# Products of constants ahead of waiting matmul groups in an attention stage with two MLPs

## The chip, the core and the metric

The kernel runs on one core of a Trainium2 chip. The metric is the device time of one execution in microseconds. A core has a tensor engine (matmul; PE in the rows, PEld for its weight loads), a vector engine (DVE), a scalar engine (ACT), a Pool engine (POOL) and a sync engine (SP), which here issues all DMAs. Matmuls write to PSUM, eight banks of 128 x 512 fp32; everything else works from SBUF. The tensor engine's clock is granted to it at one of two levels, 1.2 or 2.4 GHz.

## What is computed

Attention with normalised q and k over 4 batches, 12 heads, 448 positions and head size 64; then two MLPs on the 1792 x 768 result, the first with a squared ReLU and the second with a PReLU, each 768 to 2048 to 768.

```python
q_n, k_n = rmsnorm(q, g_q), rmsnorm(k, g_k)
scores = (1.0 / np.sqrt(64)) * np.matmul(q_n, k_n.transpose(0, 1, 3, 2))
scores = scores - np.max(scores, axis=-1, keepdims=True)
attn = np.exp(scores)
attn = attn / (np.sum(attn, axis=-1, keepdims=True) + 1e-09)
x = np.matmul(attn, v)          # brought to 1792 x 768
h = np.maximum(x @ moe_w_in, 0.0)
x = h * h @ moe_w_out
h = x @ moe2_w_in
g = np.maximum(h, 0.0) + moe2_alpha * np.minimum(h, 0.0)
return g @ moe2_w_out
```

## The kernel before

Most matmul operands are split into a high and a low part, and three products of parts stand for one fp32 product; a few products, L727 among them, are plain fp32 and run as two records each.

The order of all instructions is made by a planner, class Tasks. Every step is a task with its engine or engines, a cost in us for each, the buffers that it reads and writes, and an urgency. Tasks.run works out for each engine the task that could start soonest, by dependencies (plus a fixed delay, WAIT), by when the engine is done, and by when a buffer slot from the task's pool becomes free; among those within 0.05 us of the soonest the lowest urgency wins. Tasks marked with a gap start 0.12 us later on the vector and scalar engines. Steps of the vector engine that are not marked "free" share a port with the Pool engine in the plan, and exclude each other. The task chosen is emitted at once, so the planner's order is the program order on each engine. A slot is returned when the last task on its buffer has been emitted, with the planned end as the time from which it is free. Costs are simple formulas, such as 0.07 + 0.00104 n us for a vector operation on n columns, 0.05 + 0.00084 n for a scalar one that reads PSUM, and MM = 0.202 us for a product of 448 columns.

The attention stage (with_attention, L419) has six PSUM banks in the pool "bank" and two in "pv". It runs batches 0 and 1 with the first MLP of batches 0 and 1 woven in, then batches 2 and 3. Two of the six banks go over to the MLP's accumulators (give, L800; pool "m") once the first batch's last head has begun. The second function, without (L824), does the rest and is a planner run of its own.

In a batch, norms makes the reciprocal norms, rhl. For each pair of heads, spread (L626) brings them to all rows by a product into a bank (L634), one for k and one for q, and multiplies k or q in that bank (L639). prep (L661) copies each head's half of the bank to st (k) and mv (q) with the scalar engine (recorded at L254) and writes the low part with a subtraction on the vector engine (recorded at L262); four of these steps of each head read the two banks. shift (L677) makes four products per head into fresh banks (L683), reduces each to the row maximum mc (L687), transposes it (L690) and sends it by DMA into a row of mv. head (L697) makes the scores (L708) into fresh banks, takes the exponential (L716) into pf or hl, and multiplies with v into a bank of "pv" (L727, or L751 for the pairs in IN_PARTS); for L751 the low part hl is a subtraction that reads the scores' bank (L742, recorded at L262). norm (L758) divides: z and d are copied out of the pv bank, z by the scalar engine (L764) from one half of the partitions, d from the other (L767, recorded at L258 or L254).

columns is a 128 x 2 tile of constants, -1e-9 and 0 or -1, written at the start. The weight stream (single, L268 on) gives the vector engine steps on ws (L286 to L296), which are spread over the same time.

Of the kernel before, what the change touches and what calls it, by code (L numbers as in the profile page):

```python
# [16 lines left out]
B, H, S, D = 4, 12, 448, 64  # L17
# [8 lines left out]
NSEL = max(max(g) for g in GROUPS)  # L26
UP, DN = 384, 512
TINY = 2.0 ** -15

# [3 lines left out]
class Buf:  # L35


    def __init__(self, ap=None, pool=None):
        self.ap, self.pool, self.slot = ap, (pool,) if isinstance(pool, str) else pool, None
        self.left, self.open, self.until = 0, False, 0.0  # L40
        self.writer, self.readers = {}, {}
# [11 lines left out]
class Tasks:  # L53
# [2 lines left out]
    PRICE = {"A": 1.5, "V": 3.5, "P": 1.5}  # L56

    def __init__(self):
        self.phase = 0
        self.new, self.free, self.ends, self.last = [], {}, {e: 0.0 for e in "TAVPS"}, {}  # L60
        self.dma = self.port = 0.0
        self.gap = dict.fromkeys("TAVPS", 0.0)
# [4 lines left out]
    def add(self, urgency, on, emit, reads=(), writes=(), chain=None, after=None, free=False, off=False):  # L67

        deps, bufs = set(), []
        for kind, items in (("r", reads), ("w", writes)):
            for x in items:
                b, part = x if isinstance(x, tuple) else (x, None)
                if b not in bufs:
                    bufs.append(b)
                if part in b.writer:
                    deps.add(b.writer[part])
                if kind == "w":  # L80
                    deps.update(b.readers.get(part, ()))
        behind = [self.last[chain]] if chain in self.last else []
        if after:
            behind.append(after)
        t = Task(urgency, on, emit, bufs, deps, behind, {"P"} if free else {"P", "V"},
                 0.12 * off)
        t.phase = self.phase
        if chain:
            self.last[chain] = t
        for x in reads:  # L90
            b, part = x if isinstance(x, tuple) else (x, None)
            b.readers.setdefault(part, []).append(t)
        for x in writes:
            b, part = x if isinstance(x, tuple) else (x, None)
            b.writer[part], b.readers[part] = t, []
        for b in bufs:
            b.left += 1
        self.new.append(t)
        return t

    def run(self, phase=0):
        ready = {e: [] for e in self.ends}
        mine, self.new = [t for t in self.new if t.phase <= phase], [t for t in self.new if t.phase > phase]

        def offer(t):
            for e in t.on:
                ready[e].append(t)

        for t in mine:
            for d in (*t.deps, *t.behind):  # L110
                if d.start is None:
                    t.missing += 1
                    d.next.append(t)
        for t in mine:
            if not t.missing:
                offer(t)
        left = len(mine)
        while left:
            best = None
            for e, tasks in ready.items():  # L120
                found, soonest = [], None
                for t in tasks:
                    s = self.ends[e] + (max(t.gap, self.gap[e]) if e in "AV" else 0)
                    s = max(s, self.port) if e in t.alone else s
                    for d in t.deps:
                        s = max(s, d.end + (0 if d.engine == e == "T" else self.WAIT[e]))
                    for d in t.behind:
                        s = max(s, d.start)
                    taken = []
                    for b in t.bufs:  # L130
                        if b.ap is None:
                            taken.append(self.slot(b, taken))
                            s = max(s, taken[-1][0] + self.WAIT[e]) if taken[-1] else None
                            if s is None:
                                break
                    if s is None:
                        continue
                    if len(t.on) > 1:
                        other = min(max(self.ends[o], s, self.port if o in t.alone else 0) + self.PRICE[o] * t.on[o]
                                    + 0.7 * sum(x.on[o] for x in ready[o] if x.urgency < t.urgency)  # L140
                                    for o in t.on if o != e)
                        if s + self.PRICE[e] * t.on[e] > other + 0.2:
                            continue
                    found.append((s, t.urgency, t))
                    soonest = s if soonest is None else min(soonest, s)
                if found:
                    s, _, t = min((x for x in found if x[0] <= soonest + 0.05), key=lambda x: x[1])
                    if best is None or s < best[0]:
                        best = (s, e, t)
            assert best, "no task can start"  # L150
            s, e, t = best
            for o in t.on:
                ready[o].remove(t)
            for b in t.bufs:
                if b.ap is None:
                    _, n, b.pool = self.slot(b)
                    slots = self.free[b.pool]
                    b.slot = slots.pop(next(i for i, x in enumerate(slots) if x[1] == n))
                    b.ap = b.slot[2]
            t.engine, t.start = e, s  # L160
            if e == "S" and t.on[e]:
                self.ends[e] = s + 0.06
                self.dma = max(self.dma, s + 1.3) + t.on[e]
                t.end = self.dma + 0.8
            else:
                t.end = self.ends[e] = s + t.on[e]
                self.gap[e] = t.gap
                if e in t.alone:
                    self.port = t.end
            t.emit(e)  # L170
            left -= 1
            for b in t.bufs:
                b.left -= 1
                b.until = max(b.until, t.end)
                self.release(b)
            for n in t.next:
                n.missing -= 1
                if not n.missing:
                    offer(n)
# [19 lines left out]
def dve2(n):  # L199
    return 0.07 + 0.00052 * n  # L200
# [18 lines left out]
def attention_relu2_mlp_prelu_mlp(ctx: ExitStack, tc: tile.TileContext, qkt, qk_tm, v, gb, alpha, ident, sel,  # L219
                                  w1, w2, w3, w4, out):  # L220
    nc = tc.nc
    ts = Tasks()
# [11 lines left out]
    columns = const.tile([128, 2], F32, name="columns")  # L234
# [33 lines left out]
    def single(w, i, urgency, after=None, last=None):  # L268
# [14 lines left out]
        if last:  # L283
            last[:] = t0, t1
        add(urgency, {"V": dve2(n)},
            lambda e: nc.vector.tensor_scalar(out=f.ap[:, :n], in0=f.ap[:, :n], scalar1=TINY, scalar2=None, op0=ALU.max),  # L286
            [], [f])
# [131 lines left out]
    def with_attention():  # L419
        with ExitStack() as es:  # L420
# [61 lines left out]
            def constants(after):  # L482
# [2 lines left out]
                add(200, {"V": 0.1}, lambda e: nc.vector.tensor_scalar(out=al_b.ap, in0=al_b.ap, scalar1=-1.0, scalar2=None,  # L485
                                                                       op0=ALU.mult), [], [al_b])

            first_scores, qk_load = {}, [None]

            def attention(b, base, first=False):  # L490
# [328 lines left out]
            for u in range(cur[0], cur[0] + 3):  # L819
                prepare(u, 5000)  # L820
                made[u].open = True
            ts.run()

    def without():  # L824
        with ExitStack() as es:
# [353 lines left out]
    with tc.manual_schedule():  # L1179
        with_attention()  # L1180
        without()
# [64 lines left out]
```

## Time and profile before

| | us |
|---|---|
| median of 3 runs | 1263.94 |
| lowest and highest | 1261.74, 1265.78 |
| the profiled execution | 1261.38 |
| its span, first to last instruction | 1259.6 |
| tensor engine busy | 1177.3 |
| vector engine busy | 908.8 |
| scalar engine busy | 794.5 |

The mean granted clock of the profiled execution was 0.977 of full. Attention fills the stretch up to about 545 us. A line of the timeline gives start, length, engine, source line, operation, output and inputs, shape, count, and in brackets the idle time of that engine before it with the releaser. Merged lines cover several instructions in a row, and lengths of matmuls overlap a little. The chain of waits is followed back from the last instruction, so that its pieces lie end to end.

### The profile page before, as it was taken

What the parts mean: (1) busy time and instruction counts of PE and PEld (TensorE: products, weight loads), DVE (VectorE), ACT (ScalarE), POOL (GpSimd) and SP (SyncE); (2) the same over time, 40 slices, a digit from 0 to 9 for tenths busy, and PEclk for the clock granted to TensorE, in tenths of its full rate; (3) what the DMA queues carried; (4) which work ended last, traced back from release to release, by engine and by line L of the source; (5) the groups of instructions that cost most, each with busy time, mean ns of one, the idle gap of its engine ahead of it and who ended that gap; (6) DMA issues with size and microseconds to landing.
All of it is one profiled execution on the core that took longest, in us unless ns stands there. A gap on an engine that the chain in (4) does not pass through costs nothing.

```text
span 1259.6 us, 17375 instructions
## 1 busy us (share of the span) xinstructions
PE 1177.3 (93%) x5502; PEld 1016.9 (81%) x5502; DVE 908.8 (72%) x1632; ACT 794.5 (63%) x1596; POOL 527.3 (42%) x485
## 2 busy tenths in 40 slices
PE   4996999897999999999999999999999979999998
PEld 2554767686888888889989999888889879888988
DVE  6789999999988877613777661088777996847484
ACT  5687879787789978822555221376746755645472
POOL 4344355555555524310000003864777743317355
PEclk7997999898999999999999999999999989999999
DMA  6136657798645633358998996572617448161632
GB/s 189 55 117 218 226 192 252 253 309 296 241 150 167 221 132 121 110 182 269 315 335 296 340 358 215 187 266 92 236 62 263 160 162 252 57 201 50 204 110 88
DMA packets 95803, 250.32 MB, mean 199 GB/s; under 512 B 11296, under 2 KB 30880, under 8 KB 95712
## 3 DMA queue, kind: packets, MB, share of 16 engines
q1 hardware_dynamic: 95712, 249.22, 58.6%
q8 instruction: 43, 0.70, 0.2%
q14 instruction: 48, 0.39, 0.1%
HBM read 178.32 MB, written 70.78 MB: 198 GB/s over the span
## 4 chain that ended last, share of the span: by engine, by line
PE 63%; DVE 17%; ACT 9%; DMA 6%; issue 4%; SPq 1%; POOL 0%; ACTq 0%; DVEq 0%; POOLq 0%
PE n L982 26%; PE m L350 14%; PE bank L350 10%; PE bank L708 4%; PE pv L751 4%; PE pv L727 3%; DMA raw<-in_w 3%; DVE mc L687 2%; PE bank L683 2%; DVE ws L293 2%; DVE ws L296 2%; DVE n L993 1%; DMA whl<-w 1%; DVE ws L286 1%; DMA tm<-in_qk_tm 1%
## 5 line engine op out<-in xcount | busy, mean ns | idle before, releaser
L982 PE MATMUL n<-forms,whl 128*128 128x448 f32 x1008 | 212.1, 371 | 17.2 <-ACT ws L254 7.2
L982 PEld LDWEIGHTS n<-forms,whl 128*128 128x128 f32 x1008 | 190.7, 190 | 37.6 <-DVE forms L262 8.2
L350 PE MATMUL bank<-xs,whl 128*128 128x448 f32 x576 | 138.4, 373 | 1.1 <-DMA whl<-w 1.1
L350 PE MATMUL bank<-hg,whl 128*128 128x448 f32 x576 | 130.5, 370 | 2.6 <-DMA whl<-w 1.9
L982 PE MATMUL n<-xs,whl 128*128 128x448 f32 x576 | 124.2, 369 | 4.0 <-DMA whl<-k_u 2.8
L282 ACT ACTIVATE ws<-raw 128x384 f32<-128x384 f32 (+1 forms) x112 | 67.3, 601 | 95.3 <-DMA raw<-in_w 84.7
L982 PEld LDWEIGHTS n<-xs,whl 128*128 128x128 f32 x576 | 109.1, 190 | 14.1 <-DMA whl<-k_u 3.2
L350 PE MATMUL m<-xs,whl 128*128 128x448 f32 x576 | 118.0, 366 | 1.6 <-DMA whl<-w 0.9
L350 PEld LDWEIGHTS bank<-hg,whl 128*128 128x128 f32 x576 | 109.1, 191 | 12.7 <-DMA whl<-w 2.2
L350 PEld LDWEIGHTS bank<-xs,whl 128*128 128x128 f32 x576 | 108.6, 191 | 12.9 <-DMA whl<-w 1.7
L687 DVE TENSOR_REDUCE mc<-bank 112x1 f32<-112x448 f32 x192 | 111.5, 616 | 8.8 <-PE bank L683 7.5
L350 PEld LDWEIGHTS m<-xs,whl 128*128 128x128 f32 x576 | 107.9, 188 | 11.7 <-ACT q L254 1.1
L350 PE MATMUL m<-hg,whl 128*128 128x448 f32 x576 | 116.9, 365 | 0.0
L262 POOL TENSOR_TENSOR whl<-ws,whl 128x384 fp32r<-128x384 f32 (+2 forms) x57 | 80.5, 1422 | 83.3 <-ACT whl L254 61.1
L350 PEld LDWEIGHTS m<-hg,whl 128*128 128x128 f32 x576 | 108.2, 188 | 8.6
L262 POOL TENSOR_TENSOR whl<-raw,whl 128x384 fp32r<-128x384 f32 (+1 forms) x87 | 89.9, 1037 | 50.8 <-ACT whl L254 42.8
L262 POOL TENSOR_TENSOR xs<-q,xs 128x448 fp32r<-128x448 f32 x11 | 13.3, 1213 | 229.1 <-DMA q<-y 226.8
L708 PE MATMUL bank<-mv,st 128*128 128x448 f32 (+2 forms) x352 | 100.8, 392 | 6.5 <-DVE hl L262 2.9
L286 DVE TENSOR_SCALAR ws<-ws 128x384 f32<-128x384 f32 (+1 forms) x112 | 47.6, 427 | 81.7 <-ACT ws L282 81.5
L254 ACT ACTIVATE whl<-raw 128x384 fp32r<-128x384 f32 (+1 forms) x123 | 60.7, 500 | 56.0 <-PE n L982 43.1
L982 PE MATMUL n<-xt,whl 128*128 128x448 f32 x432 | 93.7, 366 | 1.7 <-DVE q L993 1.2
L262 DVE TENSOR_TENSOR hl<-bank,hl 128x448 fp32r<-128x448 f32 (+1 forms) x120 | 73.8, 619 | 27.8 <-ACT bank L716 25.4
(172 smaller groups left out, 2373.0 us busy)
## 6 DMA issues: line engine op xcount, KB each, us to landing
raw<-in_w SPq DMA_DIRECT2D x64, 384.0 KB
raw<-in_w SPq DMA_DIRECT2D x48, 512.0 KB
whl<-w SPq DMA_DIRECT2D x64, 384.0 KB
whl<-w SPq DMA_DIRECT2D x48, 512.0 KB
k_u<-whl SPq DMA_DIRECT2D x56, 384.0 KB
whl<-k_u SPq DMA_DIRECT2D x56, 384.0 KB
w<-whl SPq DMA_DIRECT2D x32, 384.0 KB
w<-whl SPq DMA_DIRECT2D x24, 512.0 KB
```

The costliest lines, as they stand in the source:

```text
L254: nc.scalar.activation(out=o, in_=i, func=ACTF.Copy)
L262: (nc.gpsimd if e == "P" else nc.vector).tensor_tensor(out=o, in0=x, in1=hi, op=ALU.subtract)
L282: lambda e: nc.scalar.activation(out=f.ap[:, :n], in_=half(1).bitcast(F32), func=ACTF.Abs), [raw], [f], "f")
L286: lambda e: nc.vector.tensor_scalar(out=f.ap[:, :n], in0=f.ap[:, :n], scalar1=TINY, scalar2=None, op0=ALU.max),
L293: lambda e: nc.vector.scalar_tensor_tensor(out=fu(), in0=half(1), scalar=0xC0000000, in1=fu(), op0=ALU.bitwise_and, op1=ALU.bitwise_or), [ ...
L296: lambda e: nc.vector.scalar_tensor_tensor(out=fu(), in0=half(0), scalar=29, in1=fu(), op0=ALU.logical_shift_right, op1=ALU.bitwise_or), [ ...
L350: nc.tensor.matmul(out=acc.ap[:, t, :S], lhsT=w.ap[:, part * n + 128 * kk:part * n + 128 * kk + 128], rhs=src(h, k0 + kk, t)[1](), start=( ...
L687: lambda e, t=t, pm=pm: nc.vector.reduce_max(out=mc.ap[:, t:t + 1], in_=pm.ap[:CP, :S], axis=AX.X),
L708: nc.tensor.matmul(out=pa.ap[:keys, :S], lhsT=s.ap[:rows, k, c:c + keys], rhs=m.ap[:rows, k, :], start=(k == 0), stop=(k == 1))
L727: lambda e, n=n, pfv=pfv, keys=keys: nc.tensor.matmul(out=o.ap[:, :S], lhsT=vs[p].ap.bitcast(F32)[:keys, 192 * n + 64 * j:192 * n + 64 * j ...
L751: nc.tensor.matmul(out=o.ap[:, :S], lhsT=l, rhs=r, start=(n == 0 and x == 0), stop=(half and x == 1))
L982: nc.tensor.matmul(out=psum(x), lhsT=w.ap[:, part * n + 128 * kk:part * n + 128 * kk + 128], rhs=get(h)[1](), start=fresh and h == 1, stop ...
```

## The change

The planner calls a function fill just before it emits a task of the tensor engine, if the planned start lies more than 1.5 us after the planned end of that engine's last task. The function looks whether the task has just taken a slot of the pools bank or pv. If so it issues products of the constants tile with itself into that slot: two columns on the stationary side, 448 moving columns that repeat the same two, plain fp32, two output rows. There are as many as fit into the planned gap less 0.6 us at 0.76 us each, or at 1.52 us ahead of the very first task. Their results are not read, and the group that follows starts its own accumulation in the same bank. Nothing is removed or moved; fill is switched off before the second function runs.

```diff
+FILL_LEAST, FILL_REST = 1.5, 0.6
...
-        self.phase = 0
+        self.phase, self.fill = 0, None
...
+            fresh = [b for b in t.bufs if b.ap is None]
             for b in t.bufs:
                 if b.ap is None:
                     _, n, b.pool = self.slot(b)
                     slots = self.free[b.pool]
                     b.slot = slots.pop(next(i for i, x in enumerate(slots) if x[1] == n))
                     b.ap = b.slot[2]
+            if e == "T" and self.fill and s - self.ends[e] > FILL_LEAST:
+                self.fill(fresh, self.ends[e], s)
             t.engine, t.start = e, s
...
+            def fill(bufs, since, until):
+                bank = next((b for b in bufs if b.pool in ("bank", "pv")), None)
+                if bank:
+                    for _ in range(int((until - since - FILL_REST) / (0.76 if since else 1.52))):
+                        nc.tensor.matmul(out=bank.ap[:2, :S], lhsT=columns, rhs=columns[:, None, :].to_broadcast([128, S // 2, 2]),
+                                         start=True, stop=True)
+
+            ts.fill = fill
...
             ts.run()
+            ts.fill = None
```

## Rows read from the trace of the kernel before

**Rows 1.** The page: busy time of each engine, and granted clock in 40 slices.
```profile
PE 1177.3 (93%) x5502; PEld 1016.9 (81%) x5502; DVE 908.8 (72%) x1632; ACT 794.5 (63%) x1596; POOL 527.3 (42%) x485
...
PEclk7997999898999999999999999999999989999999
```
**Rows 2.** Waits of PE, 0 to 660 us: waiter, releaser, total us, times, longest.
```profile
PE bank L634 <- DVE rhl L549: 7.9, 1, 7.9
PE bank L683 <- DVE mc L687: 6.2, 2, 5.9
...
PE bank L683 <- POOL mv L256: 3.7, 2, 2.1
PE bank L708 <- DVE mc L687: 3.1, 4, 2.2
...
PE bank L708 <- DVE hl L262: 2.9, 2, 2.6
PE bank L683 <- DVE hl L262: 2.5, 1, 2.5
```
**Rows 3.** Stretches: busy us (count) of PE, PEld, DVE, ACT, POOL; clock; DMA.
```profile
12.00:18.00 6.00, 0.00 (x0) 0.00 (x0) 5.78 (x11) 4.69 (x9) 0.00 (x0) 0.76 0.84 243
...
24.00:30.00 6.00, 4.67 (x11) 2.75 (x12) 5.92 (x13) 2.45 (x8) 0.56 (x1) 0.50 0.10 39
30.00:36.00 6.00, 6.00 (x21) 3.70 (x20) 4.09 (x10) 1.95 (x6) 0.00 (x0) 0.82 0.01 2
...
120.00:126.00 6.00, 4.93 (x17) 4.15 (x18) 5.23 (x10) 2.19 (x5) 1.18 (x2) 0.64 0.55 190
```
**Rows 4.** Chain of waits from 0 to 60 us: start, length, engine, line, count.
```profile
54.06 3.02 PE pv L727 x8
```
**Rows 5.** Timeline of PE, 0 to 130 us, the first long waits.
```profile
4.80 3.35 PE L527 MATMUL bank<-pf,hg 128*128 128x448 f32 x4 [4.80 <-ACT pf L520]
8.67 1.77 PE L527 MATMUL bank<-pf,hg 128*128 128x448 f32 x4 [0.51 <-ACT pf L520]
18.38 1.83 PE L634 MATMUL bank<-rhl,selg 128*128 128x448 f32 x4 [7.93 <-DVE rhl L549]
22.31 1.46 PE L683 MATMUL bank<-st,mv 128*112 128x448 f32 x3 [2.11 <-POOL mv L256]
```
**Rows 6.** The chain again, at half clock and, the last two, at full.
```profile
18.38 0.72 PE bank L634
...
28.73 2.24 PE bank L708 x6
30.97 0.75 PE bank L683 x2
31.71 1.05 PE pv L727 x2
...
57.49 0.81 PE bank L683 x4
58.30 1.31 PE bank L708 x6
```
**Rows 7.** Timeline of all engines around the wait that ends at 121.07 us.
```profile
108.67 1.05 PE L634 MATMUL bank<-rhl,selg 128*128 128x448 f32 x4 [0.93 <-DVE rhl L262]
...
112.84 1.15 DVE L262 TENSOR_TENSOR st<-bank,st 64x448 fp32r<-64x448 f32 x2
...
121.07 1.16 PE L683 MATMUL bank<-st,mv 128*112 128x448 f32 x2 [11.34 <-DVE st L262]
```
**Rows 8.** Waits of all engines, 105 to 126 us: the weight load of the second L683.
```profile
PEld bank L683 <- DVE mv L262: 0.2, 1, 0.2
```
**Rows 9.** Timeline of DVE: the first and the last of 23 operations in a row.
```profile
108.56 0.56 DVE L293 SCALAR_TENSOR_TENSOR ws<-raw,ws 128x384 uint32<-128x384 uint32 x1
...
120.30 0.63 DVE L262 TENSOR_TENSOR st<-bank,st 64x448 fp32r<-64x448 f32 x1
```
**Rows 10.** Timeline of all engines, 0 to 40 us: d behind z.
```profile
36.66 0.62 DVE L258 COPY d<-pv 64x448 f32<-64x448 f32 x1 [1.49 <-ACT z L764]
```

## The prediction

> **What bounds the kernel now.** I read the page's busy shares and slices first [rows 1]. The tensor engine is busy for 93% of the span, so what the change can win lies where its clock is down; the slices put that into the first 320 us, where the digits of the granted clock fall to 7 and 8. Next I read who the tensor engine waits for while attention runs [rows 2]: a few long waits, and the column to look at is the releaser, because the change treats all waits alike and the releasers are of two kinds. "L634 <- DVE rhl" and "L683 <- POOL mv" are waits for an operand. "L683 <- DVE mc", "L708 <- DVE mc", "L708 <- DVE hl" and "L683 <- DVE hl" are waits for a bank: mc is what the reduction of L687 writes and hl what the subtraction of L742 writes, and a product of L683 or L708 reads neither; both only read a PSUM bank that the next product needs. Third, the clock by stretches [rows 3]: it stands at 0.50, the lower of its two levels (1.2 and 2.4 GHz), from about 15 us until 32.2 us (0.82 over 30 to 36 is 2.2 us at half), and again from the wait that ends at 121.07 us until 124.3 us (0.64 over 120 to 126 is 28%, 1.7 us, at full).
>
> **The price of one added product.** No row shows a product with a two-column stationary side. The nearest is L727, also plain fp32 with 448 moving columns: eight records, which are four products, take 3.02 us of the chain [rows 4], 0.755 us each at full clock, and twice that, 1.51 us, at half. The code's own 0.76 and 1.52 agree. Its lower bound is half of this, should the narrow side save a pass; I keep 0.755.
>
> **How many, and where they stand.** The condition looks at the planner's own gap, s minus the end of the tensor engine's last task, and s is raised both by late operands and by the moment at which a slot becomes free. The products are written into the slot just taken, so on the chip they can start only once that bank is released. In an operand wait with a free bank they fill the gap; in a bank wait they start when the gap is over and delay the group by their whole length. Products on the m buffers (L350) get none.
>
> (a) Start. The first product waits 4.80 us [rows 5]; (4.80 - 0.6)/1.52 gives 2, 3.0 us long in an idle engine. Cost 0; if they ran over by some tenths, the second pair of products still starts at 8.67 us, after its square.
>
> (b) L634 at 18.38 us, operand wait, banks free. The planner's costs add up to 5.73 us (five vector steps of 0.536 + 0.17, three scalar ones of 0.47 + 0.17, 0.27 for the engine), so 6 products; by the trace's 7.93 us [rows 5] it would be 9. They take 4.5 to 6.8 us and end by 17.3 us, before L634 is due. Cost 0.
>
> (c) L683 at 22.31 us: operand wait of 2.11 us [rows 5], 1 or 2 products, 1.5 us at most, hidden under the copy on the Pool engine. Cost 0. If (b) and (c) hold the clock up, what follows runs at full speed. On the chain between 18.4 and 32.2 us [rows 6], L634 goes from 0.72 to 0.37, six records of L708 from 2.24 to 1.31, two of L683 from 0.75 to 0.40 (four take 0.81 at full), two of L727 from 1.05 to 0.76: 0.35 + 0.93 + 0.35 + 0.29 = 1.9 us. Most of the rest of that stretch is vector and scalar work that does not care. I take -1.7, with ends at -0.35 (only L634 passes on) and -4.
>
> (d) L683 at 121.07 us, the longest wait, 11.34 us, released by "DVE st" [rows 7]. Is it operand or bank? Batch 1 has just spread two pairs into four banks (L634 at 108.67 us, four products), the pool holds six less the two handed to the MLP, so none is free. Head 0's own half of st was written at 112.84 us, and st at 120.30 us is head 1's: the first two subtractions into st are the j=0 heads of both pairs, since j=1 tasks carry a gap of 0.12 us and lose each choice to whatever can start sooner. That subtraction is the last reader of the key bank, which the first L683 takes. The next L683 then waits for the following "mv" subtraction, the last reader of the query bank [rows 8], as it must if banks are the limit. So this is a bank wait, and the planner has it too: from the second L262 into rhl the 23 vector operations from 108.56 to 120.30 us [rows 9] cost 11.4 us by its formulas, plus 0.27, less the 1.08 us until its four L634 are done: 10.6 us, hence int(10.0/0.76) = 13 products; waits for the shared port can only add, and the trace's 11.34 gives 14. They start at 121.0 us with the clock at half. As it took 3.2 us to come back after 121.07, two run at half and eleven at full: 3.2 + 11 x 0.755 = 11.5 us. Queued behind them on the tensor engine are L683 and the MLP's L350; for L683 waits the vector engine's next instruction (L687), for L350 the scalar engine's (L386). Nothing hides it. Given back: the 3.2 us that ran at half clock now run at full, 1.6 us. Net +9.9; ends +8.5 (some catching up) and +13.
>
> (e) The smaller bank waits: 2.6, 2.5, 2.2 and 5.9 us [rows 2]. Were they in the plan at this size, they would get 2, 2, 2 and 6 products: 12 x 0.755 = 9.1 us, plus 1.5 for two at half clock, less some 2 regained, about 8.5 us. They need not be in it: they may come from the vector engine running behind its plan. Bounds 0 and +9; I take half, +4, since the trace is the nearest view of the plan there is.
>
> **Does the bank really hold them?** The products write partitions 0 and 1 only. The row that decides is DVE L258 [rows 10]: copying partitions 0 to 63 of a pv bank into d it waited 1.49 us for ACT L764, which read partitions 64 to 127 of the same bank into z; the two share nothing else. Accesses to one bank by two engines are therefore ordered whatever their partitions. The Trainium skill (PSUM — Partial Sum Buffer, PSUM bank collisions raise a hardware error) says that two engines may use a bank at once if they are in different quadrants of 32 partitions, though it calls guarding by whole bank the simple version; by quadrants the third case below would come true, but the trace shows whole banks here.
>
> **Sum.** -1.7 + 9.9 + 4 = +12.2 us. On the profiled execution (1261.38 us, of which 1259.6 are span) this is 1273.6; against the median of 1263.94, 2.6 us above it, 1276. I give 1276, with 1268 to 1286 for this case: -4 + 8.5 + 0 and -0.35 + 13 + 9.
>
> **Rivals.**
> Narrow products leave the clock low. Nothing in the trace shows what two columns of constants do to it. Then (c) wins nothing and (d) costs 13 x 1.51 = 19.6 with nothing regained; with half of (e), six at 1.51, 9 us: about 1290, from 1284.
> Products held by their own two partitions only. In (d) they would start when head 0's subtraction ends at 113.4 us [rows 7], run 11.5 us to 124.9, 3.9 us past the release; less 1.6 regained and 1.7 from (c) that is about +0.6, so 1264.5, no change. Against it: rows 10.
> The waits are filled as named. If the bank in (d) were free early, or the plan's gap there short, only gains are left: -1.7 at the start, -1.6 after 121 us, and 1.5 or so for the half-clock spells that follow the later waits: 1259, faster. It decides by whether the tensor engine's first added product in (d) runs near 110 us or at 121 us. The Trainium skill (TensorE: Matmul & The Clock Gate, Why this matters for your kernels) advises to leave no idle gaps between bursts of matmuls so that the clock stays up; by that rule alone this would be the result. It prices no wait of the filling work itself.
>
> **How the numbers follow.** Forecast 0.66, clock stays low 0.10, held by partitions 0.14, filled as named 0.10. A measurement of this kernel can tell about 0.3%, 3.8 us, from no change, so the bounds are 1260.1 and 1267.7. Faster: most of the last case and a little of the third, 0.09. Same: the rest of both and the low edge of the forecast, 0.15. Slower: 0.76. The range from 1264 to 1292 leaves out the last case, part of the third and the top of the second, just under 0.2.
>
> **What would show it.** In the profile after: two-partition products in a train of 13 or 14 that starts at 121 us and not at 110, with the group of L683 about 11 us later and L687 and L386 idle as long; granted clock 1.00 over 18 to 30 us and PE busy there without L634 moving later; a train also behind some of the bank waits of (e). I am wrong if the train in (d) lies inside the wait, if its products take 0.2 us, or if the vector engine catches up the delay before 330 us.

## The result, and the profile after

The changed kernel takes 1278.54 us (median of 4 runs, 1275.54 to 1280.71) against 1262.84 us for the kernel before, measured beside it: a ratio of 1.0128, 95% interval 1.01 to 1.0155. It is slower by 15.7 us; 1276 us was forecast. The profiled execution took 1280.71 us, with a span of 1278.9.

In its lines the steps of attention stand 12 lines lower than before: L634 is L646, L683 is L695, L708 is L720, L727 is L739. Lines ahead of attention stand 4 lower: L262 is L266, L350 is L354, L386 is L390. The added product is L496. There are 34 of them, 68 records. First, all trains in the timeline of PE of the changed kernel: start, length, engine, line, operation, count, and in brackets the wait before it.

```profile
1.81 3.15 PE L496 MATMUL bank<-columns 128*2 128x448 f32 x4 [1.81 <-DVE columns L459]
...
10.46 6.96 PE L496 MATMUL bank<-columns 128*2 128x448 f32 x18
18.38 1.05 PE L646 MATMUL bank<-rhl,selg 128*128 128x448 f32 x4 [0.96 <-DVE rhl L561]
19.36 1.67 PE L496 MATMUL bank<-columns 128*2 128x448 f32 x4
...
121.88 12.27 PE L496 MATMUL bank<-columns 128*2 128x448 f32 x26 [11.24 <-DVE st L266]
134.08 0.66 PE L695 MATMUL bank<-st,mv 128*112 128x448 f32 x2
...
233.76 1.65 PE L496 MATMUL bank<-columns 128*2 128x448 f32 x2 [3.45 <-DVE hl L266]
...
256.68 0.92 PE L496 MATMUL bank<-columns 128*2 128x448 f32 x2 [2.16 <-DVE mc L699]
...
312.97 7.01 PE L496 MATMUL bank<-columns 128*2 128x448 f32 x12 [8.08 <-DVE mc L699]
319.91 0.46 PE L695 MATMUL bank<-st,mv 128*112 128x448 f32 x1
```

Two records are one product, so the trains have 2, 9 and 2 products, then 13, then 1, 1 and 6. The first three begin when the constants are written or the engine falls idle (10.46 us is the end of the pair before). The first delays its group by 0.1 us, from 4.80 us [rows 5] to 4.89; the other two are over before their group is due, and L646 starts at 18.38 us as it did [rows 5]. The other four carry in brackets a wait of the kind that used to stand ahead of the group [rows 2, 7], two of them longer than before (3.45 us for 2.6, 8.08 us for 5.9): 11.24 us of it before the 13 products, which then keep L695 away for another 12.2 us, to 134.08 instead of 121.07 us.

Who pays is in the same timeline, other engines:

```profile
134.58 1.16 DVE L699 TENSOR_REDUCE mc<-bank 112x1 f32<-112x448 f32 x2 [12.21 <-PE bank L695]
...
135.39 0.54 ACT L390 ACTIVATE q<-bank 128x448 f32<-128x448 f32 x1 [15.28 <-PE bank L354]
```

The vector engine stood idle for 12.21 us before its next reduction. On the page its whole group of reductions waited 26.0 us for L695, where they waited 7.5 us for L683 before; the line of before, then that of the changed kernel:

```profile
L687 DVE TENSOR_REDUCE mc<-bank 112x1 f32<-112x448 f32 x192 | 111.5, 616 | 8.8 <-PE bank L683 7.5
L699 DVE TENSOR_REDUCE mc<-bank 112x1 f32<-112x448 f32 x192 | 111.1, 615 | 27.1 <-PE bank L695 26.0
```

Lining up the vector engine's operations of the two traces, its work is 0.9 us later than before at 40 to 113 us (times of the kernel before), 12.0 at 150 to 187 us, 18.2 at 300 to 310 us, 21.0 at 346 to 396 us and 19.3 at the end. The last figure belongs to these two executions (1280.71 and 1261.38 us); between medians it is 15.7.

### The profile page after: what moved, and what is told of

It reads as the page before. It is cut to its first block, busy times and chain, and to the rows that moved or that the text cites. A ratio compares the mean times of both kernels' runs of the same rounds, so it can differ in the third digit from the quotient of the medians.

```text
span 1278.9 us, 17509 instructions
## 1 busy us (share of the span) xinstructions
PE 1208.4 (94%) x5570; PEld 1018.3 (80%) x5570; DVE 909.2 (71%) x1632; ACT 792.5 (62%) x1596; POOL 519.5 (41%) x485
## 4 chain that ended last, share of the span: by engine, by line
PE 68%; DVE 14%; ACT 9%; DMA 4%; issue 3%; POOL 0%; SPq 0%; DVEq 0%; ACTq 0%; POOLq 0%
PE n L995 24%; PE m L354 19%; PE bank L354 10%; PE bank L720 4%; PE pv L763 4%; PE pv L739 3%; PE bank L695 2%; DVE mc L699 2%; PE bank L496 2%; DMA tm<-in_qk_tm 2%; DVE n L1006 1%; DMA raw<-in_w 1%; DVE raw L919 1%; DVE ws L297 1%; DVE ws L300 1%
## 5 line engine op out<-in xcount | busy, mean ns | idle before, releaser
L995 PE MATMUL n<-forms,whl 128*128 128x448 f32 x1008 | 212.6, 371 | 17.4 <-ACT ws L258 7.2
L354 PE MATMUL bank<-xs,whl 128*128 128x448 f32 x576 | 137.9, 372 | 1.3 <-DMA whl<-w 1.2
L354 PE MATMUL bank<-hg,whl 128*128 128x448 f32 x576 | 128.4, 365 | 1.4 <-DMA whl<-w 0.7
L354 PE MATMUL m<-hg,whl 128*128 128x448 f32 x576 | 119.2, 368 | 0.0
L354 PE MATMUL m<-xs,whl 128*128 128x448 f32 x576 | 118.1, 367 | 0.7 <-ACT q L258 0.7
L266 POOL TENSOR_TENSOR whl<-ws,whl 128x384 fp32r<-128x384 f32 (+2 forms) x57 | 75.0, 1323 | 107.4 <-ACT whl L258 79.7
L354 PEld LDWEIGHTS bank<-xs,whl 128*128 128x128 f32 x576 | 108.1, 190 | 12.6 <-DMA whl<-w 1.6
L354 PEld LDWEIGHTS m<-hg,whl 128*128 128x128 f32 x576 | 108.1, 188 | 10.9
L354 PEld LDWEIGHTS m<-xs,whl 128*128 128x128 f32 x576 | 107.9, 188 | 10.8 <-ACT q L258 1.1
L354 PEld LDWEIGHTS bank<-hg,whl 128*128 128x128 f32 x576 | 107.2, 188 | 11.4 <-DMA whl<-w 1.5
L266 POOL TENSOR_TENSOR whl<-raw,whl 128x384 fp32r<-128x384 f32 (+1 forms) x87 | 89.7, 1034 | 52.2 <-ACT whl L258 44.3
L266 POOL TENSOR_TENSOR xs<-q,xs 128x448 fp32r<-128x448 f32 x11 | 13.2, 1212 | 229.1 <-ACT xs L258 229.1
L720 PE MATMUL bank<-mv,st 128*128 128x448 f32 (+2 forms) x352 | 100.9, 392 | 3.6 <-DVE rhl L266 2.8
L266 DVE TENSOR_TENSOR hl<-bank,hl 128x448 fp32r<-128x448 f32 (+1 forms) x120 | 73.7, 618 | 26.9 <-ACT bank L728 24.4
```

The source lines that it names most:

```text
L266: (nc.gpsimd if e == "P" else nc.vector).tensor_tensor(out=o, in0=x, in1=hi, op=ALU.subtract)
L354: nc.tensor.matmul(out=acc.ap[:, t, :S], lhsT=w.ap[:, part * n + 128 * kk:part * n + 128 * kk + 128], rhs=src(h, k0 + kk, t)[1](), start=( ...
L720: nc.tensor.matmul(out=pa.ap[:keys, :S], lhsT=s.ap[:rows, k, c:c + keys], rhs=m.ap[:rows, k, :], start=(k == 0), stop=(k == 1))
L995: nc.tensor.matmul(out=psum(x), lhsT=w.ap[:, part * n + 128 * kk:part * n + 128 * kk + 128], rhs=get(h)[1](), start=fresh and h == 1, stop ...
```

## Experiments

The control comes first, since it says how the other ratios are to be read. All ratios are against the kernel before on the same chip. A ratio and its interval are computed from all runs of both kernels and need not be the quotient of the two medians; a difference in us that is said to be by the ratio is worked out from it. The expectations call the theory of the forecast the bank theory: a train in the bank that its group waits for runs after the wait and adds its length.

**The change with no product issued.** It is the program of before, written as the changed kernel with an empty loop.

```diff
-                    for _ in range(int((until - since - FILL_REST) / (0.76 if since else 1.52))):
+                    for _ in range(0):
```

> The change with no product issued: the same program as before, as a control of how far two medians of one program lie apart. One product behind the longest wait came out at 0.9974 of before though its group started 1.6 us later; if that is chance, this control too may lie 1 to 3 us from before: ratio 0.997 to 1.003. If it lies within 0.0005, the 0.9974 was an effect of that product.

Measured: 1264.08 us (12 runs), 1.0025, interval 1.0001 to 1.0049. Two sets of runs of one program lay 0.25% apart by the ratio (0.18% by the medians, 1264.08 and 1261.8 us), and even the interval leaves out 1, so no ratio between 0.997 and 1.003 is read as an effect below.

**Only the products of the first 50 us.**

```diff
-                if bank:
+                if bank and since < 50:
```

> Only the products of the first 50 us of the plan are kept (2, 9 and 2 of them). Bank theory: they stand before operand waits with a free bank, so they lie inside the waits; the offset that the changed kernel had at 38 us in its trace, 0.9 us late, is all that is left: about 1263.7 us, same. Rival, every product costs its own length wherever it stands: 13 products, 2 at 1.51 and 11 at 0.755 us, 11 us late, about 1274.

Measured: 1259.12 us, 0.999 (0.9967 to 1.0013). Its 13 products, 11.3 us by their prices, cost nothing that can be told where the bank is free. The rival falls.

**Only the 13 products of the longest wait**, and then 26 of them.

```diff
-                if bank:
+                if bank and 50 < since < 150:
...
+                    for _ in range(2 * int((until - since - FILL_REST) / (0.76 if since else 1.52))):
```

> Only the 13 products before the group that waits longest (121 us) are kept. Bank theory: they run after the wait, and the vector engine's later work shifts by 11.1 us, as it did across that place in the changed kernel's trace: about 1274 us. Rival, the loss comes from the other places and this one is caught up by 330 us: below 1267.

> As the run with the longest wait alone, with 26 products in place of 13. Bank theory: the delay is the length of the train, so 13 more at full clock add 13 x 0.755 = 9.8 us: about 1284 us. Rival, what costs is the added wait itself or the clock at its start and not the length: the same time as with 13.

Measured: with 13, 1273.69 us, 1.0092 (1.0059 to 1.0124), as expected; with 26, 1279.42 us, 1.0129 (1.0102 to 1.0156). The two trains, from each timeline of PE, the first with 13 and the second with 26:

```profile
123.09 11.84 PE L496 MATMUL bank<-columns 128*2 128x448 f32 x26 [11.24 <-DVE st L266]
```
```profile
121.04 21.68 PE L496 MATMUL bank<-columns 128*2 128x448 f32 x52 [11.26 <-DVE st L266]
```

At the place the delay is the train's length: 21.68 against 11.84 us, 9.8 more for 13 more, as expected. In the whole time 1284 was expected and 1279.4 came, 5.7 us above the single train. With intervals of some 4 us to either side that may be chance or some catching up later; these runs don't tell which. In the two profiled executions the vector engine's work with 26 is 9.7 us later than with 13 at 150 to 187 us and 7.1 us at the end, once the start is taken off, where the execution with 13 was 2.0 us late.

**One product there**, in the bank that is waited for.

```diff
-                    for _ in range(int((until - since - FILL_REST) / (0.76 if since else 1.52))):
+                    for _ in range(1):
```

> One product, not 13, in the bank that the longest wait is for. Bank theory, the delay is the train's length: one product at half clock, 1.51 us, less nothing since the clock is still down after it: the group starts 1.5 us after the release, about +1.5 us, 1.001, within what can be told from no change. Rival, the delay comes with the first product because the bank is handed over once more between the engines: most of the 11 us stays.

```profile
121.22 1.65 PE L496 MATMUL bank<-columns 128*2 128x448 f32 x2 [11.25 <-DVE st L266]
122.80 1.09 PE L695 MATMUL bank<-st,mv 128*112 128x448 f32 x2
```

The timeline of PE is as expected: the group starts 1.6 us after the release, and the vector engine's work moved by 1.5 us right behind the place and by 0.7 us at 150 to 187 us. So it isn't the first product that costs 11 us. The whole time missed: 1258.18 us, 0.9974 (0.9957 to 0.9991), where 1.001 was expected. Nothing in its trace explains a gain, and the control missed by as much the other way.

**Only the later waits**, 1, 1 and 6 products.

```diff
-                if bank:
+                if bank and since > 150:
```

> Only the products behind 150 us of the plan are kept: 1, 1 and 6, each in the bank that its group waits for. Bank theory: their trains of 1.6, 0.9 and 7.0 us (as in the changed kernel's trace) run after the waits; less what a clock already up gives back, about +4 to +8 us, and with the start and the longest wait this adds up to the change's 15.7 us: 1267 to 1271 us. Rival, the later trains are absorbed because the vector engine is behind its plan there: within 2 us of before, and the longest wait is the whole loss.

Measured: 1269.47 us, 1.0069 (1.0044 to 1.0093), +8.7 us by the ratio. The largest train, in its timeline of PE:

```profile
305.41 7.57 PE L496 MATMUL bank<-columns 128*2 128x448 f32 x12 [5.91 <-DVE mc L699]
312.91 0.46 PE L695 MATMUL bank<-st,mv 128*112 128x448 f32 x1
```

The wait is the 5.9 us of before [rows 2], and 7.57 us of products come after it. The three parts add up by their ratios to -1.3 + 11.6 + 8.7 = 19 us, against 16 for the whole change by its ratio; each carries 3 to 4 us to either side.

**All trains in a bank that is free when the gap begins**, of the same lengths. At every one of these gaps a bank of the pool "pv" was free in the plan, and all products went there.

```diff
+                spare = [x[2] for p in ("pv", "bank") for x in ts.free[p] if x[0] <= since]
-                if bank:
+                if bank and spare:
...
-                        nc.tensor.matmul(out=bank.ap[:2, :S], lhsT=columns, rhs=columns[:, None, :].to_broadcast([128, S // 2, 2]),
+                        nc.tensor.matmul(out=spare[0][:2, :S], lhsT=columns, rhs=columns[:, None, :].to_broadcast([128, S // 2, 2]),
```

> All products as in the change, but written into a bank that is free when the gap begins (a pv bank, or one of the six), not into the one that the waiting group is about to take. Bank theory: every train then starts when the gap starts and lies inside it, the group at 121 us starts where it did before, and what is left is the start's 0.9 us late less up to 1.6 us at 121 us and 1 to 2 us after the later waits: 1260 to 1264 us. Rival, the products cost their time on the tensor engine whatever bank they write: 1274 or more. Rival, two-column products do not hold the clock: it falls inside the trains, and nothing is won.

Measured: 1258.8 us, 0.9957 (0.9926 to 0.9987). Its timeline of PE (lines of attention stand one lower again, L696 for L695), and three stretches of 6 us (busy us and counts of PE, PEld, DVE, ACT and POOL, then the granted clock, the share of the DMA engines and GB/s):

```profile
109.45 9.98 PE L497 MATMUL pv<-columns 128*2 128x448 f32 x26
120.86 0.91 PE L696 MATMUL bank<-st,mv 128*112 128x448 f32 x2 [1.43 <-DVE st L266]
```
```profile
108.00:114.00 6.00, 5.54 (x17) 1.71 (x18) 5.92 (x12) 5.62 (x13) 4.56 (x5) 1.00 0.67 175
114.00:120.00 6.00, 5.43 (x15) 1.08 (x13) 6.00 (x12) 4.86 (x10) 2.16 (x3) 1.00 0.61 212
120.00:126.00 6.00, 5.12 (x24) 4.06 (x24) 5.81 (x12) 3.13 (x7) 2.12 (x3) 1.00 0.59 194
```

The same 13 products start at once, end at 119.4 us and leave 1.43 us of the wait; the clock stays at its upper level, 1.00, where it stood at 0.64 over 120 to 126 us before [rows 3]. The rival that products cost their time wherever they write falls, and so does the one that two columns don't hold the clock. With this run the bank is shown to be the cause: nothing but the bank that is written differs from the change, and 15.7 us are gone.

Whether it beats the kernel before is another matter. Once more, on another chip:

> The trains of the whole change in free banks once more, on another chip, because the control put two medians of one program 0.25% apart. If the 0.9957 of the first time is a gain and not chance, it comes out below 0.998 again; if it was chance, between 0.998 and 1.002.

Measured: 1258.45 us, 0.9985 (0.9957 to 1.0013). That lies in the range named for chance; a gain of 0.2 to 0.4% is neither shown nor excluded.

**The longest wait alone, in a free bank**, with 13 products and with one.

```diff
+                if bank and spare and 50 < since < 150:
...
+                    for _ in range(1):
```

> The 13 products of the longest wait alone, in a free bank. Against the same 13 in the bank that the group waits for (1.0092 of before) this moves nothing but the bank. Bank theory: the train starts within 0.2 us of the end of the four products before it, ends before 121 us, the clock does not fall there, and the vector engine's work after it is 0 to 1.6 us earlier than in before: 1260.5 to 1262, 0.999. Rival, 13 products cost 10 us on the tensor engine wherever they write: 1.008 or more.

> One product at the start of the longest wait, in a free bank, where it can neither delay the group nor hold the clock for 11 us. If the gain of 13 products in a free bank (0.9967) comes from the held clock, this one gives nothing: 0.999 to 1.001. If it gives 0.997 as well, the gain there does not come from the clock of that wait.

Measured: 13 products 1257.89 us, 0.9967 (0.9947 to 0.9988); one product 1265.32 us, 1.0029 (1.0006 to 1.0052), the same as the control of its chip. Both lie outside the expectations (0.999, and 0.999 to 1.001), by no more than the control does. What is clear of noise is the bank: the same 13 products gave 1.0092 in the bank that the group waits for. For a gain the two lie on the sides that a held clock would give, but 13 products in a free bank and one in the waiting bank came out alike on one chip (0.9967 and 0.9974), so this is not shown. In the trace of the 13, the vector engine's work moves earlier by 0.8 us between 81 and 162 us.

**The start, held.** Products in a free bank ahead of every gap of the first 50 us above 0.4 us, rounded up; then this together with all trains in free banks.

```diff
-FILL_LEAST, FILL_REST = 1.5, 0.6
+FILL_LEAST, FILL_REST = 0.4, 0.6
...
+                if spare and since < 50:
+                    for _ in range(int((until - since - 0.2) / 0.76 + 0.5) if since else 2):
```

> Products in the first 50 us of the plan alone, in a free bank, before every wait of more than 0.4 us and rounded up, so that few gaps are left between 18 and 28 us. If the low clock between 24 and 34 us is what keeps the start from gaining, the clock now stays up over 18 to 34 us and the vector work at 40 us comes 1.5 to 2.5 us earlier than before: about 1260.5 us. Rival, the gaps there are mostly not in the plan (the vector engine runs behind it), so the clock falls near 24 us again and nothing more is won than by the first 13 products: 1261 to 1263.

> The trains of the whole change in free banks, together with the held start. If the gains add: 4 us for the free banks and up to 2 for the start, about 1257 us, 0.995 of before or less. Rival, the clock's falls move to other places and the sum is that of the free banks alone: 1258 to 1259.

Measured: 1260.7 us, 0.9995 (0.9972 to 1.0018), and 1258.42 us, 0.9971 (0.9944 to 0.9997), where the gains do not add: the rival's range came. The clock does stay up in both, from 6.8 to 112.6 us in the first and from 5.9 to 326.8 us in the second. By the stretches of the second kernel:

```profile
24.00:30.00 6.00, 5.75 (x20) 2.23 (x20) 5.92 (x12) 2.31 (x8) 0.39 (x1) 1.00 0.09 36
30.00:36.00 6.00, 6.00 (x26) 3.70 (x24) 4.58 (x12) 3.00 (x7) 0.00 (x0) 1.00 0.02 5
```

and its chain of waits shows the gain of the start, which the next section compares (L720, L695 and L739 stand 5 lines lower here):

```profile
28.89 1.25 PE bank L725 x6
30.14 0.40 PE bank L700 x2
30.54 0.76 PE pv L744 x2
```

The vector work at 40 us came 1.5 us earlier than in before in this trace. In that of the start alone it came 0.5 us later, where 1.5 to 2.5 us earlier was expected; there the second pair of q and k was used only at 10.3 us, 2.3 us later than in before. A gain of the start is in one trace of two, and in whole times it is below what can be told.

## Why the prediction was right, and where a term was off

**Bank or operand.** This step carried the forecast, and it held. The train in (d) began at 121.88 us behind "DVE st", not near 110. It also settles the case in which two partitions alone hold the products: head 0's subtraction ended at about 114.4 us in this trace, and the train began 7.5 us later, behind the subtraction that the forecast took for head 1's:

```profile
113.75 1.15 DVE L266 TENSOR_TENSOR st<-bank,st 64x448 fp32r<-64x448 f32 x2
...
121.20 0.62 DVE L266 TENSOR_TENSOR st<-bank,st 64x448 fp32r<-64x448 f32 x1
```

The Trainium skill (PSUM — Partial Sum Buffer, PSUM bank collisions raise a hardware error) would allow two engines in one bank at different quadrants; this program's waits don't use that, they order accesses by the whole bank, as the row of d behind z had shown [rows 10].

**The count and the price (d).** Thirteen products by the planner's costs, and 13 came. (For (b) the same reckoning gave 6 and the trace's wait 9, and 9 came, so there the plan's gap had been reckoned too short; it cost nothing.) A product at full clock took 9.98/13 = 0.77 us in the free bank, against 0.755. The train took 12.2 us instead of 11.5, because the clock came back later: at 126.6 us, 4.7 us after the train's start, where 3.2 had been read from the kernel before. That the narrow products are the reason is not shown, since it was up 3.8 us after the start of the train in each of the runs with 13 and 26 products at this place alone. In the stretches of the changed kernel:

```profile
120.00:126.00 6.00, 4.12 (x6) 0.73 (x7) 2.34 (x4) 0.11 (x1) 1.83 (x2) 0.50 0.63 210
126.00:132.00 6.00, 6.00 (x16) 1.31 (x15) 0.00 (x0) 0.00 (x0) 0.34 (x1) 0.95 0.00 0
```

Given back was 1.0 us instead of 1.6: the group stood 12.1 us later against its own start (13.0 less the 0.9 of the beginning), the vector work behind it 11.1. Net +11.1 in the trace and +11.6 by the ratio of the single run, for +9.9, inside the ends that were given.

**The later waits (e): mis-sized.** The forecast took half of 8.5 us because the waits might not be in the plan. Three of the four trains came, with 8 products instead of 12, and the single run gives +8.7 us by its ratio (5.6 to 11.7): near the upper bound, +9, not at half. The largest wait, 5.9 us, was in the plan nearly whole, with 6 products, as its own formula gave. The 2.5 us wait got none. Taking the trace's waits as the plan's would have been the better choice.

**The start (c): its condition failed.** It was taken at -1.7 us on the condition that the trains hold the clock over 18 to 34 us. They hold it to 24.2 us and no further, by the stretches and the chain of waits of the changed kernel:

```profile
18.00:24.00 6.00, 3.68 (x12) 1.53 (x12) 5.66 (x11) 4.35 (x9) 2.94 (x6) 1.00 0.72 243
24.00:30.00 6.00, 4.62 (x12) 2.76 (x13) 5.92 (x12) 2.24 (x8) 0.42 (x1) 0.51 0.05 21
30.00:36.00 6.00, 6.00 (x16) 3.83 (x16) 3.83 (x10) 1.62 (x3) 0.00 (x0) 0.63 0.01 2
```
```profile
18.38 0.45 PE bank L646
...
28.46 2.24 PE bank L720 x6
30.70 0.75 PE bank L695 x2
31.45 1.49 PE pv L739 x2
```

The low stretch moved from 15.1 to 32.2 us to 24.2 to 34.4 us: out of a stretch bound by vector work, where it had cost little, and more of it into the one bound by PE. L646 took 0.27 us less, of 0.35 reckoned, but the six records of the scores took 2.24 us and the two of L695 0.75 us as before [rows 6], those of L739 1.49 instead of 1.05 us, and work at 40 us was 0.9 us later. This lateness belongs to one execution. In the three others with the same 13 products at the start (the start alone, and both runs of all trains in free banks) the clock fell at 24.7 to 25.1 us and was back by 31.5 to 31.9 us, and the vector engine's work at 40 us was 0.4 to 0.6 us earlier than in before, close to the end of -0.35 us at which only L634 passes on. The seven executions with no product at the start spread from 0.1 to 4.6 us later than that of before at the same place, so what the trains of the start won or cost is not shown. The start alone, by its stretches:

```profile
24.00:30.00 6.00, 4.60 (x13) 2.77 (x13) 5.92 (x13) 2.24 (x8) 0.23 (x1) 0.56 0.08 30
30.00:36.00 6.00, 6.00 (x23) 3.84 (x22) 3.64 (x9) 2.23 (x5) 0.00 (x0) 0.87 0.01 1
```

Its whole time, -1.3 us by the ratio with 3 us to either side, settles it no better. Held through, the same three pieces take 1.25, 0.40 and 0.76 us: the prices in the sum were right, the condition was not met. The prediction had named it ("if (b) and (c) hold the clock up") and then took it for granted. The idle stretches that are left between 21 and 28 us are 1.0 us at most in the changed kernel's trace, and a train needs 1.5 us in the plan; when 0.4 us was enough, in the run of the start held, seven products came between 21 and 31 us and the clock stayed up.

**The sum.** 12.2 us was forecast. The parts measured between 0.9 us late and 1.3 us early at the start, 11.1 to 11.6, and 8.7, and the whole 15.7 us, between 12.6 and 19.6 by its ratio. Every part came out above its term, and the measured parts add up to some 19 us. That 1276 lies only 2.5 us below the measured median is therefore in part luck. The mechanism held, and the case's own range (1268 to 1286) covers the larger sum too.

## What to carry to other kernels

Filler work inherits the wait of the buffer that it writes: before you put it ahead of a waiting group, ask whether the group waits for an operand or for that very buffer, and if the second, write somewhere that is free at the start of the gap. A wait's releaser says which it is: if the waiting product does not read what the releaser wrote, it is a buffer. Names alone can mislead here: the wait at 121 us is on "st", which the product reads, but it was another head's. And a clock that is up only matters where its engine is on the path: in the changed kernel's trace the low stretch at the start moved into work that waits for the tensor engine, so most of what the trains had bought there was paid again.

## What the runs showed of the hardware that was not expected

Products with two columns on the stationary side kept the clock up, and it came back while they ran: it held at 1.00 through 10 us of nothing else on the tensor engine (the stretches of the free banks above), and in the train at 312.97 us it rose at 317.7 us, 4.7 us after the start (0.65 in this stretch of the changed kernel is 0.3 us at full). Over the five trains of six products or more that began at the lower level (here, at 121.88 us, and in the runs with 13, 26 and the later waits alone) the rise came 3.8 to 5.9 us after the start. The stretch of the train at 312.97 us:

```profile
317.00:318.00 1.00, 1.00 (x3) 0.19 (x2) 0.00 (x0) 0.00 (x0) 0.00 (x0) 0.65 1.00 410
```

The Trainium skill (TensorE: Matmul & The Clock Gate, Why this matters for your kernels) asks for no long idle gaps between bursts of matmuls. In the longest wait the trace agrees: a train of constants in a free bank closed the gap, and the clock held at 1.00. At the start of the changed kernel short gaps were enough: the clock fell at 24.2 us, though no idle stretch of the tensor engine between 17.4 and 24.2 us was longer than 1.0 us; it had been busy for 3.68 us of the 6 from 18 to 24 us.

Unchanged parts of the program vary more than the forecast reckoned. The second pair of q and k landed between 7.8 and 10.6 us, by the squares that wait for it. The first line is from the run of the start alone, the second from that of the later waits alone, whose start is that of the kernel before:

```profile
7.77 1.04 ACT L532 ACTIVATE pf<-qk 128x448 f32<-128x448 f32 x2 [2.51 <-DMA qk<-in_qkt]
```
```profile
10.57 1.04 ACT L532 ACTIVATE pf<-qk 128x448 f32<-128x448 f32 x2 [5.14 <-DMA qk<-in_qkt]
```

The second of these executions was 4.6 us late at 40 us with no product issued yet. The falls of the clock behind attention, where no product is added, also came at other places from one execution to the next (the 8 late in the slices of before is one of them [rows 1], which the prediction's reading of the slices passed over), and behind 1000 us the profile of before lost 2 to 4 us against nine of the other thirteen. Two sets of runs of the same program can lie 0.25% apart, and a few microseconds in one trace are no evidence without a control.
